# Fused attention and gated MLP on one core: the half tile of keys fed one row group at a time

## Chip, core and metric

One NeuronCore of a Trainium2 chip runs the whole program. The metric is the device time of one execution in microseconds (us). All times of the kernel before and its trace below are of this chip.

## What is computed

```python
q_n = q / (norm(q) + 1e-6);  k_n = k / (norm(k) + 1e-6)      # (8, 12, 448, 64) each
attn = softmax(q_n @ k_n.T / tau)                            # tau = 0.1
x = (attn @ v).transpose(0, 2, 1, 3).reshape(3584, 768)
h = x @ w_in                                                 # (768, 2048)
out = (h * cos(h)) @ w_out                                   # (2048, 768)
```

There are 8 batches of 12 heads, 448 queries and keys of 64 values each. Each batch gives 448 rows of `x`, which go through the two matrix products of the MLP.

## The kernel before, in words

**Work units.** A group `g` is a pair of heads of one batch; there are 48 groups, 6 to a batch. Three groups make a unit `u` (16 units, two to a batch). The 448 keys of a head stand as 7 tiles of 64. Three pairs of tiles fill 128 partitions each; the seventh tile, the half tile of keys, has only 64 keys, so its queries are split: partitions 0 to 63 hold its keys against one half of the queries, partitions 64 to 127 the same keys against the other half.

**Scores and exponentials.** For a group, `scores(g, 0)` (L728) computes the half tile's scores, 4 matmuls of 64x64 tiles with 224 columns; `scores(g, 1)` to `scores(g, 3)` (L720) the pairs, 4 matmuls with 448 columns each. ScalarE takes each result through `exp` into the buffer `PX` (L735), which is double: group `g` uses `PX[g % 2]`, with the half tile's part in the same buffer.

**Attention product and sums.** `attend(g, direct, stages)` has three stages.
- Stage 0 and stage 1 are the half tile (`rest`, L750 to L763; I call them **R0** and **R1**). Each is 4 matmuls of 64x64 tiles with 224 columns, one in every tile of the array. R0 puts the value product of partitions 0 to 63 into one PSUM bank and, with a weight of ones, the row sums of partitions 64 to 127 into the next; R1 does it the other way round. R1 waits until R0 has finished (`settled`), because the two write the same bank from different rows of the array.
- Stage 2 is the three pairs, in tiles of 128 rows by 32 columns (**the 32-column block**): 12 matmuls for the values (`av`, L768), then for groups that are not "direct" 4 with 448 columns (`sm`, L776) and 4 with 224 columns (`sm2`, L784) for the sums. `sm2` gives each of two column tiles one half of the queries.

**Sums of groups that are not direct.** After stage 2, one copy takes values and sums to `xu` in SBUF. `chain(u)` then, once per unit: gathers the sums by two DMAs on SyncE's queue (L889), adds the two parts and takes the reciprocal on VectorE (L901, L904), writes it to DRAM ("spread", L905), reads it back to all partitions ("bcast", L907), and GpSimd multiplies the values by it (L911), which gives `xT`, the input of the first MLP product.

**MLP.** `m1(b, ...)` (L919) is the first product of batch `b` in full 128x128 tiles, followed by sine and multiply into `gT`. The second product is cut into small steps that fill the time between attention blocks: `m2_quarters` (L1017), each step 4 matmuls of 64x64 tiles with 384 columns, one in every tile of the array. Within a step the order was: for each half of the output rows `x`, first row group `z` = 0, then `z` = 1. After half of an output tile, the two row groups change PSUM banks, and the next step waits for the last one to have finished (`settled` again).

**What sets the order.** TensorE's order from group 19 on is written by hand (`PLAN["script"]`): `s20.1` is a scores step of group 20, `f4` is 4 steps of the second MLP product, `a20`, `b20`, `c20` are stages 0, 1, 2 of group 20, `m2` is the first MLP product of batch 2. Earlier groups follow `pair`. The other engines are ordered at build time by a planner (`Program.play`), which simulates all engines with costs written in the code and takes at each engine the ready operation that is due first. The array changes between three tilings: 64x64 (scores, R, second product), 128x32 (stage 2), and 128x128 (first product).

Of the kernel before, what the change touches and what calls it, by code (L numbers as in the profile page):

```python
# [6 lines left out]
ACT = mybir.ActivationFunctionType  # L7
ALU = mybir.AluOpType
F32 = mybir.dt.float32
# [9 lines left out]
    "swapped": {},  # L19
    "script": {19: """  # L20
# [8 lines left out]
        s32.1 f2 a31 f2 b31 s32.2 f5 s32.3 f7 a32 s33.0 f5 s33.1 f5 s33.2 f6 b32 c32 s33.3 f10 m4 f6  # L29
        a33 s34.0 f8 s34.1 f8 b33 c33 s34.2 f5 s34.3 f5 s35.0 f6 s35.1 f5 s35.2 f4 s35.3 f4 a34 f3 b34 s36.0 c34 c35  # L30
        s36.1 a35 f3 b35 f1 s36.2 f6 s36.3 f6 a36 s37.0 f5 s37.1 f5 s37.2 f6 b36 c36
        s37.3 f4 s38.0 f4 s38.1 f4 s38.2 f4 s38.3 f4 a37 f2 b37 s39.0 c37 c38 s39.1 a38 f3 b38 f1 s39.2 f3 s39.3 f3 m5 c39
        a39 f4 s40.0 b39 f4 s40.1 f4 s40.2 f2 s40.3 f2 s41.0 s41.1 f4 s41.2 f5 s41.3 f5 a40 f2 b40 s42.0 c40 c41
        s42.1 a41 f3 b41 f1 s42.2 f4 s42.3 f4 s43.0 f4 s43.1 f4 s43.2 f5 s43.3 f5 a42 f2 b42 s44.0 c42 c43
        s44.1 f2 a43 f2 b43 s44.2 f5 s44.3 f7 a44 s45.0 f5 s45.1 f5 s45.2 f6 b44 c44 s45.3 f10 o012 m6 f6 s46.0 a45 f12 s46.1 b45 f4 c45 s46.2 f3 s46.3 f4
# [380 lines left out]
def bass_cosine_attention__then__act_gcu_kernel(  # L416
# [13 lines left out]
    UP = 3  # L430
# [13 lines left out]
    NT = 3  # L444
    TD, LT = PLAN["turned"], 9
# [27 lines left out]
    lnn = sbs("lnn", 2, [128, UH * NB], F32)  # L473
# [4 lines left out]
    PX = sbs("PX", 2, [128, NB * S], BF16)  # L478
    xu = sb("xu", [128, 5 * UP * S], F32)
    RB = sbs("RB", 2, [128, UP * S], F32)  # L480
    sums = sbs("sums", 2, [128, 2 * SPR], F32)
    rcp = sbs("rcp", 2, [128, SPR], F32)
# [3 lines left out]
    zt = sb("zt", [128, S], BF16)  # L486
    ones = sb("ones", [128, 128], BF16)
    iot = cosb[0].bitcast(I32).ap()[:, 0:128]
# [17 lines left out]
    PXv = [t.ap()[:, 0 : NT3 * 2 * S].rearrange("p (c a s) -> p c a s", c=NT3, a=2) for t in PX]  # L506
    PHv = [t.ap()[:, NT3 * 2 * S : NB * S].rearrange("p (a s) -> p a s", a=2) for t in PX]
    xuv = xu.ap().rearrange("p (r g s) -> p r g s", r=5, g=UP)
# [15 lines left out]
    HALF = 0.096  # L524

# [49 lines left out]
    pool(lambda e: e.memset(ones.ap().rearrange("p (x y) -> p x y", y=32)[:, 0:4:3], 0.0), (), ["zeros"], 0.12)  # L575
    sel = [gT.bitcast(F32).ap()[:, (f * RING + S) // 2 : (f * RING + S) // 2 + 128] for f in (NF - 2, NF - 1)]
# [65 lines left out]
    lnnv = [t.ap().rearrange("p (h s) -> p h s", h=UH) for t in lnn]  # L642
    rnv = [t.ap().rearrange("p (h s) -> p h s", h=UH) for t in rn]

    def rnorm(u, p0, p1, t=(0, 1)):
# [5 lines left out]
        if u in PLAN["roots"] or (u, p0) in PLAN["roots"]:  # L651
# [6 lines left out]
        act(lambda e: e.activation(lnnv[i][:, h, w], n2v[i][:, h, w], ACT.Ln, bias=cst.ap()[:, 1:2]),  # L658
            [("n2", i, p, z) for p, z in keys] + ["cst1"], [("lnn", i, p, z) for p, z in keys],
            n, "E", 1, "ln" + tag)  # L660
        act(lambda e: e.activation(rnv[i][:, h, w], lnnv[i][:, h, w], ACT.Exp, scale=-0.5),  # L661
            [("lnn", i, p, z) for p, z in keys], [("rn", i, p, z) for p, z in keys], n, "E", 0, "rn" + tag)
# [47 lines left out]
    def scores(g, c, bank=None):  # L710
# [5 lines left out]
        def full(e):  # L716
            for o in range(2):
                for a in range(2):
                    r = slice(64 * a, 64 * a + 64)
                    m = e.matmul(ph[BP * o : BP * o + BP, a, 0:S], t[r, c - 1 + (NT3 + 1) * o, 0:BP],  # L720
                                 t[r, :, BP : 2 * BP], start=True, stop=True)
            return m

        def half(e):
            for o in range(2):
                for a in range(2):
# [8 lines left out]
        act(lambda e: e.activation(PHv[j] if c == 0 else PXv[j][:, c - 1], ph[:, :, 0:n], ACT.Exp, scale=1.0 / TAU),  # L735
            keys, [("PX", j, c)], 2 * n, "E", label="exp%d.%d" % (g, c))

    opened, held, turned = {}, {}, set(PLAN["swapped"])

    def attend(g, direct, stages=(0, 1, 2)):  # L740
# [8 lines left out]
        folded, swapped = g in PLAN["folded"], g in turned  # L749

        def rest(e, n):
            for k in range(2):
                o = n ^ k
                r = slice(BP * o, BP * o + BP)
                for a in range(2):
                    w = vav[y][r, 2 * p + a, 0 if o else VS - 1, :] if k == 0 else ones.ap()[r, ws]
                    to = AVq[64 * a : 64 * a + 64, k, :, o, :]
                    if folded and k:
                        w = ones.ap()[r, 64 - 64 * o : 128 - 64 * o]
                        to = av_[64 * a : 64 * a + 64, 1, 0 : S // 2]  # L760
                    m = e.matmul(to, w, PHv[j][r, a, :],  # L761
                                 start=(n == 0 and g not in PLAN["quarters"] and not swapped), stop=(n == 1 and swapped))
            return m  # L763
# [8 lines left out]
        def sm(e):  # L772
            for n in range(2):
                for a in range(2):
                    o = 64 * a + 32 * n
                    t = e.matmul(av_[o : o + 32, 1, 0:S], ones.ap()[:, 32:64], PXv[j][:, n, a, :],  # L776
                                 start=swapped, stop=False)
            return t

        def sm2(e):  # L780
            for n in range(2):
                for a in range(2):
                    o, w = 64 * a + 32 * n, slice(S // 2 * n, S // 2 * n + S // 2)
                    t = e.matmul(av_[o : o + 32, 1, w], ones.ap()[:, 32:64], PXv[j][:, 2, a, w],  # L784
                                 start=False, stop=not swapped)
            return t
# [32 lines left out]
        for n in stages:  # L819
            if n < 2:  # L820
                o = P.op("PE", lambda e, n=n: rest(e, n), [("va", y), ("PX", j, 0), "ones", "zeros"], both_keys,
# [17 lines left out]
        if not direct:  # L839
            if 2 in stages:  # L840
                P.op("PE", sm, ["ones", ("PX", j, 1), ("PX", j, 2)], [ks], cost=MM, mode="C32", label="S%d" % g)
                P.op("PE", sm2, ["ones", ("PX", j, 3)], [ks], cost=HALF, mode="C32", label="S%d" % g)
# [3 lines left out]
            both = bass.AP(xu, (u % 3 * UP + p) * S, [[5 * UP * S, 128], [(3 + i - u % 3) * UP * S, 2], [1, S]])  # L846
# [9 lines left out]
        if folded:  # L856
            s, r = xuv[:, 3 + i, p, 0 : S // 2], RBv[i][:, p, 0 : S // 2]
# [14 lines left out]
        act(lambda e: e.activation(xuv[:, 3 + i, p, :], av_[:, 1, 0:S], ACT.Ln), [ks], [("xs", i, p)], S, "E",  # L872
            label="lnS%d" % g, bias=PLAN["bs"] if g < PB else 0.0)
        act(lambda e: e.activation(r, xuv[:, 3 + i, p, :], ACT.Exp, scale=-1.0), [("xs", i, p)], [("RB", i, p)], S, "E",  # L874
# [10 lines left out]
    def chain(u):  # L885
        i, b = u % 2, u // 2
        n = sum(UP * u + p not in PLAN["direct"] for p in range(UP))
        w = SPR // UP * n
        dma("SP", [lambda e, r=r: e.dma_start(  # L889
            sums[i].ap()[:, w * r : w * r + w],  # L890
# [462 lines left out]
```

## Time and profile before

| | us |
|---|---|
| three timed executions | 420.59, 421.1, 423.0 |
| their median | 421.1 |
| the profiled execution | 420.54 |
| span of its trace | 418.8 |

The span is from the first to the last instruction of the trace; the profiled execution takes 1.7 us more than its span. A row of the timeline has start, duration, engine, line, operation, output and inputs with shapes, and the number of merged instructions. The duration of a matmul in the trace runs from its start to its modelled end, and consecutive matmuls overlap; what a block costs TensorE is the time from its start to the start of the next block.

### The profile page before, as it was taken

Reading aid. Unit: us, or ns where it says so; the run is one execution under the profiler, and the core shown is the slowest. Engines: PE = TensorE matmul, PEld = TensorE weight load, DVE = VectorE, ACT = ScalarE, POOL = GpSimd, SP = SyncE. Lnnn points to the kernel's source line nnn. Section 1 sums busy time; section 2 is a strip of 40 time slices with the busy share of each in tenths; the row PEclk is TensorE's granted clock in tenths of the full one; section 3 lists DMA queues with packets and bytes.
Section 4 is the critical chain, followed back from the end, with each engine's and each line's share of the span. In section 5 each row is a group of like instructions: output and inputs, shape, how many; then the busy total and the mean of one; then the engine's idle time right before and its main releaser. Section 6 shows DMA issues by size and latency. Waiting matters only on the chain.

```text
span 418.8 us, 13571 instructions
## 1 busy us (share of the span) xinstructions
PE 409.6 (98%) x6074; PEld 236.5 (56%) x6074; DVE 189.5 (45%) x250; ACT 271.3 (65%) x363; POOL 242.7 (58%) x193
## 2 busy tenths in 40 slices
PE   7899999999999999999999999999999999999997
PEld 3354556655556555665466555665566655565565
DVE  3564744456663277124753087213862244223421
ACT  5887578983987746877498556776498745703500
POOL 4999977989761666938864782907867320020000
PEclk9999999999999999999999999999999999999999
DMA  8999999879849997579766993949966720141023
GB/s 191 251 253 226 209 223 172 213 174 198 144 104 151 207 222 185 109 168 217 168 114 127 210 242 83 147 109 212 212 123 128 161 68 3 41 121 38 2 67 85
DMA packets 80254, 63.61 MB, mean 152 GB/s; under 512 B 44996, under 2 KB 75204, under 8 KB 80196
## 3 DMA queue, kind: packets, MB, share of 16 engines
q1 hardware_dynamic: 61988, 50.06, 55.4%
q0 software_dynamic: 18048, 12.59, 20.2%
q8 instruction: 48, 0.79, 0.8%
q10 hardware_dynamic: 160, 0.10, 0.1%
q14 instruction: 10, 0.08, 0.1%
HBM read 54.98 MB, written 11.13 MB: 158 GB/s over the span
## 4 chain that ended last, share of the span: by engine, by line
PE 92%; ACT 4%; POOL 1%; DVE 1%; DMA 1%; issue 1%; SPq 0%; ACTq 0%; POOLq 0%
PE MP L1017 27%; PE SC L919 21%; PE AV L919 11%; PE SC L720 6%; PE AV L768 4%; PE MP L1046 4%; PE SC L1046 3%; PE SC L768 2%; PE AV L761 2%; PE AV L794 2%; PE MP L919 2%; ACT PX L735 2%; PE SC L728 1%; ACT cosb L948 1%; PE MP L809 1%; PE AV L1046 1%
## 5 line engine op out<-in xcount | busy, mean ns | idle before, releaser
L735 ACT ACTIVATE PX<-SC 128x896 bf16<-128x896 f32 (+1 forms) x166 | 132.8, 828 | 26.1 <-PE SC L720 18.2
L1017 PE MATMUL MP<-W,gT 64*64 64x384 bf16 x2816 | 142.3, 324 | 0.9 <-DVE qkT L707 0.6
L1017 PEld LDWEIGHTS MP<-W,gT 64*64 64x64 bf16 x2816 | 79.2, 107 | 35.7 <-PE MP L1017 3.8
L919 PE MATMUL SC<-xT,W 128*128 128x448 bf16 x468 | 94.9, 353 | 0.0
L669 POOL TENSOR_TENSOR qks<-raw,rn 128x896 bf16<-128x896 f32 (+1 forms) x48 | 79.8, 1679 | 24.6 <-ACT rn L661 24.0
L630 POOL TENSOR_TENSOR sq<-raw 128x896 bf16<-128x896 f32 x44 | 73.6, 1692 | 9.0 <-DMA raw<-in_q_dram 7.0
L948 ACT ACTIVATE cosb<-SC,cst 128x896 f32<-128x896 f32 x39 | 39.1, 1006 | 57.0 <-PE SC L919 52.6
L911 POOL TENSOR_TENSOR xT<-xu,RB 128x448 bf16<-128x448 f32 x34 | 37.8, 1136 | 60.7 <-DMA RB<-scr 60.7
L919 PEld LDWEIGHTS SC<-xT,W 128*128 128x128 bf16 x468 | 45.5, 98 | 42.8 <-ACT xu L848 0.6
L950 DVE TENSOR_TENSOR gT<-SC,cosb 128x896 bf16<-128x896 f32 x39 | 42.4, 1089 | 40.6 <-ACT cosb L948 38.3
L919 PE MATMUL AV<-xT,W 128*128 128x448 bf16 x264 | 56.7, 353 | 0.0
L984 DVE COPY osb<-MP 128x384 f32<-128x384 f32 x50 | 25.8, 553 | 66.8 <-PE MP L1017 56.1
L637 DVE TENSOR_REDUCE n<-sq 128x14 f32<-128x896 bf16 (+2 forms) x49 | 51.2, 1058 | 6.1 <-ACT sq L628 5.3
L720 PE MATMUL SC<-qkT 64*64 64x448 bf16 x504 | 45.6, 356 | 0.6 <-ACT PX L735 0.6
L919 PEld LDWEIGHTS AV<-xT,W 128*128 128x128 bf16 x264 | 25.6, 98 | 24.2 <-ACT xu L848 0.3
L948 ACT ACTIVATE cosb<-AV,cst 128x896 f32<-128x896 f32 x22 | 22.1, 1006 | 23.6 <-PE AV L919 20.7
L950 DVE TENSOR_TENSOR gT<-AV,cosb 128x896 bf16<-128x896 f32 x22 | 23.9, 1088 | 14.3 <-ACT cosb L948 14.2
L604 POOL DMA_DIRECT2D va<-in_v_dram x32 | 21.9, 692 | 7.0 <-DMA raw<-in_q_dram 4.2
L878 POOL TENSOR_TENSOR xT<-xu,RB 128x448 bf16<-128x448 f32 x8 | 9.1, 1134 | 28.5 <-ACT RB L874 28.5
L851 DVE COPY xu<-AV 128x896 f32<-128x896 f32 x13 | 14.2, 1091 | 21.5 <-PE AV L784 14.6
L552 ACT ACT_TABLE_LOAD x17 | 21.8, 1283 | 1.0 <-PEq L1335 0.7
L720 PEld LDWEIGHTS SC<-qkT 64*64 64x64 bf16 x504 | 14.4, 106 | 14.2 <-ACT PX L735 6.1
(95 smaller groups left out, 428.0 us busy)
## 6 DMA issues: line engine op xcount, KB each, us to landing
raw<-in_k_dram SPq DMA_DIRECT2D x48, 224.0 KB, 6.5
raw<-in_q_dram SPq DMA_DIRECT2D x48, 224.0 KB, 6.7
out_dram<-osb SPq DMA_DIRECT2D x54, 192.0 KB, 3.5
va<-in_v_dram POOLq DMA_DIRECT2D x32, 192.0 KB, 7.1
RB<-scr SPq DMA_DIRECT2D x18, 336.0 KB, 4.7
W<-in_moe_w_in_dram POOLq DMA_DIRECT2D x4, 768.0 KB, 15.9
W<-in_moe_w_out_dram POOLq DMA_DIRECT2D x4, 768.0 KB, 18.6
RB<-scr SPq DMA_DIRECT2D x6, 224.0 KB, 4.0
```

The source lines that it names most:

```text
L630: pool(lambda e, x=x, y=y: e.tensor_tensor(y, x, x, ALU.mult), src_, dst, 0.1 + n * 1.78e-3, label="sq%d.%d" % (u, p)).pad = LATE if u > 1 ...
L637: dve(lambda e, w=w: e.tensor_reduce(out=n2v[i][:, 2 * p : 2 * p + 2, w], in_=sqv[p][:, :, w, :], axis=mybir.AxisListType.X, op=ALU.add), ...
L669: f = lambda e, s0=s0, s1=s1: e.tensor_tensor(qksv[i][:, p, s0:s1].rearrange("p s h d -> p h s d"), rawv[i][:, h, s0:s1, :], bass.AP(rn[i] ...
L720: m = e.matmul(ph[BP * o : BP * o + BP, a, 0:S], t[r, c - 1 + (NT3 + 1) * o, 0:BP], t[r, :, BP : 2 * BP], start=True, stop=True)
L735: act(lambda e: e.activation(PHv[j] if c == 0 else PXv[j][:, c - 1], ph[:, :, 0:n], ACT.Exp, scale=1.0 / TAU), keys, [("PX", j, c)], 2 * n ...
L911: pool(lambda e, p=p: e.tensor_tensor(xTv[b % 2][:, UP * i + p, :], xuv[:, u % 3, p, :], RBv[i][:, p, :], ALU.mult), [("RB", i, p), ("xa", ...
L919: t = e.matmul(ph[:, a, 0:S], W1v[:, order[c], 128 * n : 128 * n + 128], xTv[b % 2][:, order[c], :], start=(c == 0), stop=(c == NKC - 1))
L948: act(lambda e, ph=ph, cz=cz: e.activation(cosv[cz], ph[:, :, 0:S], ACT.Sin, bias=cst.ap()[:, 0:1], scale=1.0), names(gi) + ["cst0"], [("c ...
L950: dve(lambda e, ph=ph, cz=cz, gi=gi: e.tensor_tensor(gTv[:, 2 * gi : 2 * gi + 2, S * (b % 2) : S * (b % 2) + S], ph[:, :, 0:S], cosv[cz], ...
L984: dve(lambda e: e.tensor_copy(dst, po[:, 0:n]), name, [("osb", o, hf)], n, label="osb%d" % t)
L1017: r = e.matmul(POH[b][x : x + 64, 0:HW], gTv[k, y, col + x : col + x + 64], W2v[k, y, HW * b : HW * b + HW], start=(y == 0 and h == 0), st ...
L1046: r = e.matmul(po[:, 0 : w[1] - w[0]], gTv[:, y, col : col + 128], W2v[:, y, w[0] : w[1]], start=(y == 0), stop=(y == NF - 1))
```

## The change

From unit 7 on (`"alone": range(7, 16)`), for the 25 groups that are not direct (21, 22, and 24 to 46), the two half-tile stages do only the value product: R0 is now 2 matmuls on partitions 0 to 63, R1 is 2 matmuls on partitions 64 to 127. The half tile's sums move to the 32-column block: a new weight `tail` (128x32: 16 columns of ones for each row group) gives the sums of both row groups in one matmul of 224 columns per head, in the column tile that used to take one half of the third pair. The third pair is redistributed, 336 columns to one column tile and 112 to the other.

```diff
+        def row(e, o):
+            r = slice(BP * o, BP * o + BP)
+            for a in range(2):
+                m = e.matmul(AVq[64 * a : 64 * a + 64, 0, :, o, :], vav[y][r, 2 * p + a, 0 if o else VS - 1, :], PHv[g % 3][r, a, :],
+                             start=(o == 0 and not swapped), stop=(o == 1 and swapped))
+            return m
         def sm(e):
+            w = ones.ap()[:, 80:112] if alone else ones.ap()[:, 32:64]
-                    t = e.matmul(av_[o : o + 32, 1, 0:S], ones.ap()[:, 32:64], PXv[j][:, n, a, :],
-                                 start=swapped, stop=False)
+                    t = e.matmul(av_[o : o + 32, 1, 0:S], w, PXv[j][:, n, a, :], start=alone or swapped, stop=False)
+        def sm2(e):
+            for a in range(2):
+                e.matmul(AVq[64 * a + 32 : 64 * a + 64, 1, :, 0, :], tail.ap(), PHv[g % 3][:, a, :], start=False, stop=False)
+            for a in range(2):
+                e.matmul(av_[64 * a : 64 * a + 32, 1, 0:SH], ones.ap()[:, 80:112], PXv[j][:, 2, a, 0:SH], start=False, stop=True)
+            for a in range(2):
+                t = e.matmul(av_[64 * a + 32 : 64 * a + 64, 1, SH:S], ones.ap()[:, 80:112], PXv[j][:, 2, a, SH:S],
+                             start=False, stop=True)
+            return t
+            if n < 2 and alone:
+                o = P.op("PE", lambda e, n=n: row(e, n), [("va", y), ("PH", g % 3)], [ka], cost=HALF - 0.006 if n else 0.008,
+                         mode="Q", label="R%d" % g)
+                if n:
+                    P.settled(opened[g], o)
```

Here `SH` is 336. The old `sm2` stays as `sm1` for the other groups. The sums of the second row group now lie in partitions 48 to 63 of each 64, in the places of the first half of the queries. A third gather DMA reads them, shifted by 32 columns (two zeroed gaps in `xu` make the shift safe), and the addition runs over three parts:

```diff
-            bass.AP(xu, (32 * r * 5 + 3 + i) * UP * S, [[64 * 5 * UP * S, 2], [w, 64], [1, w]]))
-            for r in range(2)], [("xs", i, p) for p in range(n)], [("sums", i)], "sums%d" % i, 0.7,
+            sums[i].ap()[:, w * r : w * r + w], bass.AP(xu, x, [[64 * XW, 2], [w, 64], [1, w]]))
+            for r, x in enumerate((XS[i], 32 * XW + XS[i], 48 * XW + XS[i] - HQ)[:m])], ["gap"] + [("xs", i, p) for p in range(n)], [("sums", i)], "sums%d" % i, 0.7,
```

For all groups, the order inside a step of 64x64 tiles becomes row group 1 (partitions 64 to 127) first, then row group 0:

```diff
-            for o in range(2):
-                for a in range(2):
+            for a in (1, 0):
+                for o in range(2):
...
-                for x in range(0, 128, 64):
-                    for z in range(2):
+                for z in (1, 0):
+                    for x in range(0, 128, 64):
```

The half tile's exponentials get a buffer of their own with three copies (`PH[g % 3]`). To make room, the buffer `lnn` goes (the logarithm is written to `rn`), `rcp` becomes single, and the zeros for the warm-up matmuls lie in an output buffer. Five small memsets are added at the start on VectorE. In the hand-written order four places change:

```diff
-        s32.1 f2 a31 f2 b31 s32.2 f5 s32.3 f7 a32 s33.0 f5 s33.1 f5 s33.2 f6 b32 c32 s33.3 f10 m4 f6
-        a33 s34.0 f8 s34.1 f8 b33 c33
+        s32.1 f2 a31 f2 b31 s32.2 f5 s32.3 f2 a32 f5 b32 s33.0 f5 s33.1 f5 s33.2 f6 c32 s33.3 f10 m4 a33 f6
+        b33 s34.0 f8 s34.1 f8 c33
...
-        a39 f4 s40.0 b39 f4 s40.1 f4 s40.2 f2 s40.3 f2 s41.0 s41.1 f4 s41.2 f5 s41.3 f5
+        a39 f4 s40.0 b39 f4 s40.1 f4 s40.2 f4 s40.3 f2 s41.0 f2 s41.1 f3 s41.2 f3 s41.3 f4
...
-        s44.1 f2 a43 f2 b43 s44.2 f5 s44.3 f7 a44 s45.0 f5 s45.1 f5 s45.2 f6 b44 c44 s45.3 f10 o012 m6 f6 s46.0 a45 f12 s46.1 b45 f4 c45
+        s44.1 f2 a43 f2 b43 s44.2 f5 s44.3 f4 a44 f3 b44 s45.0 f5 s45.1 f5 s45.2 f6 c44 s45.3 f10 o012 m6 a45 f6 b45 s46.0 f12 s46.1 f4 c45
```

More of the change, by code (lines that the diff above doesn't have):

```diff
@@ L19 @@
     "swapped": {},
+    "alone": range(7, 16),
     "script": {19: """
@@ L444, in bass_cosine_attention__then__act_gcu_kernel @@
     NT = 3
+    XS = [UP * S * (3 + i) + HQ * (i + 1) for i in range(2)]
+    XW = XS[1] + UP * S
     TD, LT = PLAN["turned"], 9
@@ L724, in half @@
         def half(e):
[L725 to L726 removed]
+            for a in (1, 0):
+                for o in range(2):
                     r = slice(64 * a, 64 * a + 64)
@@ L747, in attend @@
         ws = slice(32, 96) if direct else slice(64, 128)
-        folded, swapped = g in PLAN["folded"], g in turned
+        folded, swapped, alone = g in PLAN["folded"], g in turned, not direct and u in PLAN["alone"]
         def rest(e, n):
@@ L841, in attend @@
                 P.op("PE", sm, ["ones", ("PX", j, 1), ("PX", j, 2)], [ks], cost=MM, mode="C32", label="S%d" % g)
-                P.op("PE", sm2, ["ones", ("PX", j, 3)], [ks], cost=HALF, mode="C32", label="S%d" % g)
+                if alone:
+                    P.op("PE", sm2, ["ones", "tail", ("PH", g % 3), ("PX", j, 3)], [ks], cost=0.15, mode="C32", label="S%d" % g)
+                else:
+                    P.op("PE", sm1, ["ones", ("PX", j, 3)], [ks], cost=HALF, mode="C32", label="S%d" % g)
             if swapped and 1 not in stages:
```

85 lines of the change are left out of this document (46 added, 39 removed).

## The prediction

> **What bounds the kernel now.** I read the page first: the share of the engines, the granted clock, and the chain that ended last.
>
> ```profile
> span 418.8 us, 13571 instructions
> ...
> PE 409.6 (98%) x6074; PEld 236.5 (56%) x6074; DVE 189.5 (45%) x250; ACT 271.3 (65%) x363; POOL 242.7 (58%) x193
> ...
> PEclk9999999999999999999999999999999999999999
> ...
> PE 92%; ACT 4%; POOL 1%; DVE 1%; DMA 1%; issue 1%; SPq 0%; ACTq 0%; POOLq 0%
> ```
>
> TensorE works in 98% of the span at full clock, and it is 92% of the last chain. In the part that the change touches, a stage table has no hole at all:
>
> ```profile
> 164.00:189.00 25.00, 24.96 (x596) 15.83 (x592) 7.66 (x12) 20.95 (x31) 15.62 (x12) 1.00 0.69 150
> 189.00:236.00 47.00, 47.00 (x792) 27.75 (x788) 22.51 (x29) 34.24 (x45) 32.24 (x24) 1.00 0.84 163
> ```
>
> The first two numbers after the stage are its length and TensorE's busy time. So from unit 7 on the time is a plain sum of what each block costs TensorE, and the change is worth what it takes from this sum, unless it makes a wait. Costs of blocks come from the timeline, as the distance between starts. The first row ends group 25's 32-column block; then come group 26's block and its half tile:
>
> ```profile
> 186.79 0.27 PE L784 MATMUL SC<-PX,ones 128*32 128x224 bf16 x4
> 186.88 0.74 PE L768 MATMUL AV<-PX,va 128*32 128x448 bf16 x12
> 187.45 0.36 PE L776 MATMUL AV<-PX,ones 128*32 128x448 bf16 x4
> 187.64 0.27 PE L784 MATMUL AV<-PX,ones 128*32 128x224 bf16 x4
> 187.84 0.38 PE L720 MATMUL SC<-qkT 64*64 64x448 bf16 x4
> 188.05 0.33 PE L1017 MATMUL MP<-W,gT 64*64 64x384 bf16 x4
> 188.22 0.26 PE L761 MATMUL AV<-PX,va 64*64 64x224 bf16 x1
> ...
> 188.31 0.49 PE L1017 MATMUL MP<-W,gT 64*64 64x384 bf16 x8
> 188.64 0.26 PE L761 MATMUL AV<-PX,ones 64*64 64x224 bf16 x1
> ...
> 188.73 0.36 PE L720 MATMUL SC<-qkT 64*64 64x448 bf16 x4
> ```
>
> Read the starts. 187.45 to 187.64: 448 columns cost 0.19, so a column costs 0.42 ns. 188.31 to 188.64: two steps of 384 columns cost 0.33. R0 (188.22) and R1 (188.64) cost 0.09 each, which is 224 columns: 0.095. The 224 columns of `sm2` cost 0.09 before another block of the same tiling (186.79) and 0.20 before a change of tiling (187.64), so a change costs 0.11.
>
> **The change part by part.**
>
> *The half tile.* R0 and R1 used all four tiles for 0.095 each. Now each uses one row group. R0 occupies row group 0 for 0.095, while the next step can enter row group 1 at once; from there row group 0 runs 0.095 behind, until R1 occupies row group 1 for 0.095 and they are level. If the row groups can part, the pair costs 0.095 and not 0.19. The trace of before has no lag of this size; the nearest rows are these:
>
> ```profile
> 110.75 0.39 PE L720 MATMUL SC<-qkT 64*64 64x448 bf16 x4
> 110.94 0.26 PE L761 MATMUL AV<-PX,ones 64*64 64x224 bf16 x1
> 110.97 0.26 PE L761 MATMUL AV<-PX,va 64*64 64x224 bf16 x1
> ```
>
> One tile starts its part of a block 0.03 before the others start theirs, so tiles are not tied together. I take the full saving: 25 groups x 0.095 = 2.38 less. The two added starts stand in the queue ahead of the next step; starts in a block lie some 0.0035 apart (four of them within 0.01 at 188.22), so 25 x 0.007 = 0.18 back. From above the bound is no saving at all (rival 2).
>
> *The sums.* The column tile that gets `tail` runs 224 + 112 = 336 columns, the other 336 at once, where both ran 224. That is 112 columns, 0.047, and two more starts, 0.007: 25 x 0.054 = 1.35 more. The weights of the 112 columns could be late; a weight load takes 0.11, which would be 25 x 0.11 = 2.7 at most. The nearest row is against it: at 186.79 to 186.88 new weights followed 224 columns in the same 32-column tiles without a gap. I take 0. From below, it can't be less than the columns. The number of changes of tiling is the same in both orders of TensorE's instructions (106), so those cancel.
>
> *R1's wait.* R1 waits for R0's end. The weight loads show when it is released:
>
> ```profile
> PEld AV L761 <- PE AV L761: 2.2, 10, 0.2
> 188.22 0.21 PEld L1017 LDWEIGHTS MP<-W,gT 64*64 64x64 bf16 x8
> 188.55 0.11 PEld L761 LDWEIGHTS AV<-PX,va 64*64 64x64 bf16 x2
> ```
>
> In this window of two steps, R1's weights came 0.33 after R0's start, 0.09 before TensorE reached R1 at 188.64, which hid the load. Now the leading row group reaches R1 0.33 after R0, just when the load begins. Queued behind R1 are its own matmuls and the next scores step, whose exponential ScalarE waits for. The cost lies between 0 and a load of 0.11; a load that begins late costs 0.02 at 187.84 to 188.05 (0.21 where 448 columns take 0.19). I take 0.035. Of the 25 windows between R0 and R1, 9 have two steps: 9 x 0.035 = 0.3 (bounds 0 and 1.0). With three steps or more the load is in time.
>
> *Windows that lose the lag.* Any wait of the whole array between R0 and R1 lets the lagging row group catch up, and then R1 costs its full 0.095. One window (group 36) has a change of banks of the second product inside, which waits for the lagging row group: 0.1. Four more have scores inside; no wait of before stands there long enough to count.
>
> *Order inside a step.* Row group 1 first, for scores and the second product. R0 and R1 already went row group by row group and cost exactly their columns, so 0.
>
> *The gather.* A third DMA on SyncE's queue, in 9 units. The case with least room is unit 7, for batch 3's first product:
>
> ```profile
> 174.51 1.18 SPq L889 DMA_DIRECT2D sums<-xu  x2
> 177.49 1.23 SPq L686 DMA_TRANSPOSE qkT<-qks  x1
> 178.77 0.58 SPq L905 DMA_DIRECT2D scr<-rcp  x1
> 180.75 1.18 SPq L988 DMA_DIRECT2D out_dram<-osb  x2
> 181.98 1.23 SPq L907 DMA_DIRECT2D RB<-scr  x2
> 177.33 0.24 DVE L904 RECIPROCAL rcp<-rcp 128x14 f32<-128x14 f32 x1
> 189.93 2.22 POOL L911 TENSOR_TENSOR xT<-xu,RB 128x448 bf16<-128x448 f32 x2 [8.11 <-DMA RB<-scr]
> 193.09 0.54 PE L919 MATMUL AV<-xT,W 128*128 128x448 bf16 x2
> ```
>
> One more gather is 1.18 / 2 = 0.59. The reciprocal would end at 177.57 + 0.6 = 178.2, and its spread stands behind the transpose until 178.72 anyway. The read-back stands behind an output whose place the change does not move. So 0 here, and were all 0.6 passed on, the second `xT` would end at 192.15 + 0.6, before its matmul at 193.09. In other units the delay passes through, but they have more room. Past the gather, the transposes and loads behind it move by 0.6. The addition over three parts is a few hundredths. The price if this cover goes is rival 3.
>
> *The start.* Five memsets come before the first reduction; they are off the path:
>
> ```profile
> 0.89 0.06 DVE L572 MEMSET cst<- 128x1 f32 x1
> 1.59 0.24 DVE L1075 MEMSET zt<- 128x224 uint32 x1
> 5.94 0.70 DVE n L637
> ```
>
> Five times 0.06 moves the zeros from 1.83 to 2.1; the first link of VectorE in the last chain is at 5.94, behind the first load. Cost 0. Sharing `rcp` and `rn` adds order between operations that already lie in order; a third half-tile buffer can only take waits away. 0 for both.
>
> **Sum.** -2.38 + 0.18 + 1.35 + 0.3 + 0.1 = -0.45, against the profiled execution's 420.54 (span 418.8 and 1.7 around it): 420.1. The median of the runs shown, 421.1, is 0.56 above the profiled one; on its footing the forecast is 421.1 - 0.5 = **420.6**. Twice as many columns leave the half tile as come to the sums (224 against 112), but small terms eat half of it.
>
> **Rivals.**
>
> 1. *The forecast*, 420.6; its own range, with the terms' nearer bounds (-0.85 with nothing lost, +0.3 with late weights in all nine) and the scatter of the runs, is 419.6 to 421.6. Chance 0.64.
>
> 2. *The change does not do what it says: row groups do not part.* A step would wait for R0 in all tiles. The pair costs 0.19 as before, the sums and starts still cost 1.35 + 0.18: 421.1 + 1.5 = 422.6. For it: no lag over 0.03 is in the trace. Against it: 0.03 is there. Chance 0.10.
>
> 3. *The sums come late to the first product (slower).* Place: SyncE and GpSimd between gather and `xT`, units 7 and 11. It decides once the second `xT` of unit 7 is over 193.09 - 192.15 = 0.94 later. The gather alone does not do that; a further GpSimd instruction pushed ahead does:
>
> ```profile
> L669 POOL TENSOR_TENSOR qks<-raw,rn 128x896 bf16<-128x896 f32 (+1 forms) x48 | 79.8, 1679 | 24.6 <-ACT rn L661 24.0
> 285.05 3.32 POOL L911 TENSOR_TENSOR xT<-xu,RB 128x448 bf16<-128x448 f32 x3 [13.14 <-DMA RB<-scr]
> 289.90 0.35 PE L919 MATMUL SC<-xT,W 128*128 128x448 bf16 x1
> ```
>
> With 1.68 + 0.6, batch 3 waits 1.3, and batch 5, whose room is 289.90 - 288.37 = 1.5, waits 0.8: 420.6 + 2.1 = 422.7; a second such push would make it 425. For it: GpSimd's order of these two kinds does change, in later units. Against it: there the first product is further off. Chance 0.13.
>
> 4. *Weights of the lagging row group can't load during R0.* In the rows above, second-product weights began to load at 188.22, as R0 entered the same tiles, and the step started at 188.31, so they do. If they did not, each window would pay a load of 0.107 (the second product's mean) in the row group that sets the end: 25 x 0.107 = 2.7, hence 420.6 + 2.7 = 423.3. Chance 0.03. The Trainium skill, TensorE: Matmul & The Clock Gate, Part 3 (What overlaps and what doesn't), says that weight loads overlap matmuls in flight only where the row group differs; by that rule this rival would hold, and the trace disagrees.
>
> 5. *More than the sum.* Nothing lost (-0.85), and the third half-tile buffer removes some of TensorE's waits for exponentials:
>
> ```profile
> PEld SC L720 <- ACT PX L735: 6.1, 20, 0.5
> ```
>
> This is idle time of weight loads, most of it hidden; a tenth of it would be 0.6: 421.1 - 1.5 = 419.6. Chance 0.10.
>
> **How the numbers follow.** The likeliest is 420.6. The range takes rival 5 with some scatter below, rivals 2 and 3 above: 419.0 to 422.9; rival 4 and a doubled rival 3 stay out. About 0.5%, 2.1 us, is what a measurement of this kernel can tell from no change. Faster by more needs rival 5 and then some: 0.08. Slower by more needs rival 4, or the upper part of 2 and 3: 0.13. Within: 0.79.
>
> **What would show it.** Right: after R0 (two matmuls) the next step's rows come split, two and two, 0.09 apart, until R1; `sm2`'s block costs 0.25 to the next start where it cost 0.20; in windows of two steps R1's weights start as its matmuls do. Wrong: a step starting whole 0.09 after R0 (rival 2); holes on TensorE ahead of the first product at batches 3 or 5 (rival 3); 112-column matmuls starting over 0.11 after the `tail` ones.

## The result, and the profile after

| | before | after |
|---|---|---|
| median of 21 runs each, us | 421.1 (420.56 to 423.0) | 420.51 (420.09 to 421.71) |
| ratio, with its 95% interval | | 0.9982 [0.9974, 0.999] |
| the profiled execution, us | 420.54 | 421.53 |
| its span, us | 418.8 | 419.7 |

The change made the kernel 0.6 us faster by the medians; the interval of the ratio makes it 0.4 to 1.1. The forecast was 420.6. The two profiled executions say the opposite (419.7 against 418.8), and that has to be settled first. The page of after:

```profile
span 419.7 us, 13486 instructions
...
PE 410.3 (98%) x6024; PEld 240.4 (57%) x6024; DVE 190.1 (45%) x255; ACT 271.6 (65%) x363; POOL 242.8 (58%) x193
...
PE 92%; DMA 4%; ACT 2%; DVE 1%; issue 0%; POOL 0%; SPq 0%; ACTq 0%
```

TensorE still works in 98% of the span. But DMA is 4% of the last chain, where it was 1%. The longest piece of that chain says why (start, duration, what):

```profile
6.35 11.97 DMA va<-in_v_dram
```

One load of values took 12 us, at the very start, before any group that the change alters. So I cut each trace at the first matmul of batch 2's first product. Up to there, from the start of the span, four profiled executions of the two kernels took 143.91 and 143.56 (before), 145.22 and 143.77 (after): the start varies by 1.5 us for one and the same kernel. From there on almost nothing varies. I call the time from that matmul to the start of the last one **the stage**. It took 271.58 and 271.57 in before, 271.25 and 271.25 in after. The stage is a far sharper meter than the times, and it says that the change brings **0.33 us** there.

Where in the stage? The stage table of before, by batches (columns: stretch, its length, TensorE's busy time and matmuls, then the other engines), one line a batch, the last from batch 6's first product to the end of the span:

```profile
143.91:190.06 46.15, 46.11 (x753) 26.68 (x749) 20.93 (x27) 32.39 (x43) 29.86 (x26) 1.00 0.87 178
190.06:237.00 46.94, 46.94 (x789) 27.84 (x785) 22.51 (x29) 34.16 (x44) 33.11 (x25) 1.00 0.84 163
237.00:286.11 49.11, 49.11 (x837) 29.18 (x833) 21.42 (x27) 31.41 (x40) 26.53 (x20) 1.00 0.80 153
286.11:333.35 47.24, 47.05 (x788) 27.80 (x784) 22.75 (x29) 34.01 (x44) 34.24 (x27) 1.00 0.83 164
333.35:418.80 85.45, 82.39 (x740) 47.29 (x736) 28.26 (x38) 29.47 (x32) 6.66 (x6) 1.00 0.22 55
```

The same of the second trace of after:

```profile
143.77:189.94 46.17, 46.12 (x742) 27.35 (x738) 20.93 (x27) 32.40 (x43) 30.71 (x26) 1.00 0.90 180
189.94:236.92 46.98, 46.98 (x776) 28.57 (x773) 22.52 (x29) 34.24 (x44) 31.44 (x23) 1.00 0.81 157
236.92:285.98 49.06, 49.06 (x825) 29.96 (x821) 21.61 (x27) 31.29 (x40) 28.28 (x23) 1.00 0.81 159
285.98:332.96 46.98, 46.98 (x777) 28.59 (x773) 22.71 (x29) 34.04 (x44) 33.45 (x26) 1.00 0.83 166
332.96:418.30 85.34, 82.31 (x736) 47.78 (x732) 28.41 (x38) 29.42 (x32) 7.27 (x7) 1.00 0.22 55
```

If 25 half tiles each saved the same, the gain would lie evenly. It doesn't: +0.02, +0.04 and -0.05 in the first three batches, then -0.26 in one, and -0.07 from there to the last matmul (the last lines run on to the end of the span). And in the batch with -0.26 before had a hole (47.24 long, 47.05 busy) that after has not. The hole is here, in before:

```profile
308.82 0.27 PE L728 MATMUL AV<-qkT 64*64 64x224 bf16 x4
309.27 0.38 PE L720 MATMUL SC<-qkT 64*64 64x448 bf16 x4 [0.19 <-ACT PX L735]
```

A scores step starts 0.45 behind a half tile's scores that cost 0.1: it waits for ScalarE's exponential. In after, two steps of the second product stand between them (`s41.0 f2 s41.1`, where before had `s41.0 s41.1`). That is the redistributed line of the hand-written order, and not the half tile at all.

The half tile itself did on the array what the prediction said. Group 26 in after, TensorE's timeline (the group whose rows of before the prediction shows):

```profile
188.92 0.31 PE L809 MATMUL AV<-PX,ones 128*32 128x336 bf16 x1
188.93 0.26 PE L807 MATMUL AV<-PH,tail 128*32 128x224 bf16 x1
188.93 0.31 PE L809 MATMUL AV<-PX,ones 128*32 128x336 bf16 x1
188.93 0.26 PE L807 MATMUL AV<-PH,tail 128*32 128x224 bf16 x1
189.02 0.22 PE L811 MATMUL AV<-PX,ones 128*32 128x112 bf16 x2
189.17 0.38 PE L730 MATMUL SC<-qkT 64*64 64x448 bf16 x4
189.38 0.49 PE L1052 MATMUL MP<-W,gT 64*64 64x384 bf16 x6
189.56 0.26 PE L778 MATMUL AV<-PH,va 64*64 64x224 bf16 x2
189.65 0.49 PE L1052 MATMUL MP<-W,gT 64*64 64x384 bf16 x6
189.88 0.28 PE L778 MATMUL AV<-PH,va 64*64 64x224 bf16 x2
189.97 0.37 PE L730 MATMUL SC<-qkT 64*64 64x448 bf16 x4
```

From 188.92 to 189.17 the sums cost 0.25 where before had 0.20. R0 (189.56, now two matmuls) lies inside a run of three steps, one ahead of it and the two of the window: six matmuls of the second product from 189.38, R0, six more. The step in which R0 falls is split two and two, its second half 0.10 behind its first (189.55 and 189.65; the view merges the first half into the row at 189.38). From 189.38 to the next scores step at 189.97 it is 0.59; in before, 188.05 to 188.73, it was 0.68.

I added up all stretches of the stage, each from the first matmul of one tiling to the first of the next. The 32-column blocks grew by 1.23 us (25 x 0.049). The 64x64 stretches shrank by 1.56. The stretch of the hole shrank by 0.345, and its like two batches earlier, where the order did not change, by 0.045; I put the difference, 0.30, down to the line of the order. Full tiles: 0. So the half tile saved 1.26, the sums cost 1.23, and the line of the order brought 0.30.

### The profile page after: what moved, and what is told of

It is laid out like the page before. It is cut to its first block, busy times and chain, and to the rows that moved or that the text cites. A ratio compares the mean times of both kernels' runs of the same rounds, so it can differ in the third digit from the quotient of the medians.

```text
span 419.7 us, 13486 instructions
## 1 busy us (share of the span) xinstructions
PE 410.3 (98%) x6024; PEld 240.4 (57%) x6024; DVE 190.1 (45%) x255; ACT 271.6 (65%) x363; POOL 242.8 (58%) x193
## 4 chain that ended last, share of the span: by engine, by line
PE 92%; DMA 4%; ACT 2%; DVE 1%; issue 0%; POOL 0%; SPq 0%; ACTq 0%
PE MP L1052 28%; PE SC L954 21%; PE AV L954 11%; PE SC L730 6%; PE AV L785 4%; PE MP L1081 4%; DMA va<-in_v_dram 3%; PE SC L1081 3%; PE SC L785 2%; PE AV L821 2%; PE MP L954 2%; PE AV L771 1%; PE SC L738 1%; PE AV L730 1%; PE MP L836 1%; PE AV L1081 1%
## 5 line engine op out<-in xcount | busy, mean ns | idle before, releaser
L745 ACT ACTIVATE PX<-SC 128x896 bf16<-128x896 f32 x125 | 112.3, 918 | 19.7 <-PE SC L730 17.2
L1052 PEld LDWEIGHTS MP<-W,gT 64*64 64x64 bf16 x2816 | 83.1, 107 | 34.2 <-PE MP L1052 4.8
L745 ACT ACTIVATE PH<-SC 128x448 bf16<-128x448 f32 x39 | 21.3, 546 | 4.8 <-PE SC L738 4.4
L887 DVE COPY xu<-AV 128x896 f32<-128x896 f32 x12 | 13.1, 1092 | 20.5 <-PE AV L801 8.8
```

The source lines that it names most:

```text
L745: act(lambda e: e.activation(PHv[g % 3] if c == 0 else PXv[j][:, c - 1], ph[:, :, 0:n], ACT.Exp, scale=1.0 / TAU), keys, [("PX", j, c) if ...
L1052: r = e.matmul(POH[b][x : x + 64, 0:HW], gTv[k, y, col + x : col + x + 64], W2v[k, y, HW * b : HW * b + HW], start=(y == 0 and h == 0), st ...
```

## The experiments

All compare with the changed kernel's stage, 271.25, and the kernel before's, 271.58. Stretches that an edit does not touch agree between runs within some 0.01 us.

| kernel | median, us | ratio to before, 95% interval | stage, us |
|---|---|---|---|
| f1, before again | 420.3 (one run) | | 271.57 |
| f2, after again | 420.09 (one run) | | 271.25 |
| g1, before with the new line | 420.44 | 0.9992 [0.9981, 1.0003] | 271.27 |
| g2, after with the old line | 420.72 | 0.9991 [0.9982, 0.9999] | 271.49 |
| e1, order inside a step as before | 420.29 | 0.9987 [0.9978, 0.9996] | 271.31 |
| e2, four tiles | 422.21 | 1.003 [1.0016, 1.0044] | 272.65 |
| e3, no `tail` | 419.95 | 0.9976 [0.9965, 0.9986] | 270.39 |
| e4, paired scores | 422.11 | 1.0033 [1.002, 1.0046] | 273.21 |
| e5, hand-over filled | 419.72 | 0.9974 [0.9965, 0.9984] | 270.70 |
| e6, three steps | 420.15 | 0.9982 [0.9973, 0.9991] | 271.11 |
| e7, e5 and e6 | 419.72 | 0.9975 [0.9962, 0.9988] | 270.49 |
| e8, two gathers | 420.5 (one run) | | 271.74 |

**e1: does the new order inside a step do the work?** All three 64x64 loops get their old order back, the rest of the change stays.

```diff
-            for a in (1, 0):
-                for o in range(2):
+            for o in range(2):
+                for a in range(2):
...
-                for z in (1, 0):
-                    for x in range(0, 128, 64):
+                for x in range(0, 128, 64):
+                    for z in range(2):
```

> The changed kernel with the order inside a step of 64x64 tiles as before (scores: output half outside, head inside; second product: x outside, z = 0 then z = 1 inside). Theory A, matmuls start strictly in the order of the program: a step behind R0 now begins with a matmul of row group 0, which must wait 0.095 for R0 and holds up those of row group 1 behind it, so no lag builds up, the pair costs 0.19 again and most of the half tile's saving goes: 1.5 to 2.4 us more than the changed kernel, 422 to 423. Theory B, each row group takes its matmuls in its own order: the order inside a step does not matter, 420.5 within 0.4, and the split of steps after R0 stays in the trace.

The stage is 271.31, 0.06 more. TensorE's timeline of e1 still shows the split around R0:

```profile
178.74 0.26 PE L738 MATMUL SC<-qkT 64*64 64x224 bf16 x2
178.75 0.26 PE L778 MATMUL AV<-PH,va 64*64 64x224 bf16 x2
178.84 0.33 PE L1052 MATMUL MP<-W,gT 64*64 64x384 bf16 x2
178.84 0.26 PE L738 MATMUL SC<-qkT 64*64 64x224 bf16 x2
```

The half scores' one row group starts with R0, the other 0.10 later, beside the next step's first half. Each row group takes its own matmuls in its own order, so the order between row groups is worth next to nothing.

**e2: is the split what saves?** Two idle matmuls are put back into R0 and R1, on the other row group, so that each uses four tiles again (some sums are counted twice, and R0 and R1 again wait for both banks of their block, as in before).

```diff
+            r = slice(BP - BP * o, 2 * BP - BP * o)
+            for a in range(2):
+                m = e.matmul(AVq[64 * a : 64 * a + 64, 1, :, 1 - o, :], ones.ap()[r, 64:128], PHv[g % 3][r, a, :],
+                             start=(o == 0 and not swapped), stop=(o == 1))
```

> The changed kernel with two idle matmuls of 224 columns put back into R0 and R1 on the other row group, so that all four tiles are occupied again, while the sums stay in the 32-column block (some sums are counted twice in the groups that do the sums first). Theory: the saving is that of the row groups parting; what the trace shows of it after the changed kernel's losses, 1.56 us, comes back: 422.0 (421.5 to 422.9). Rival, the gain came from the new order of the other engines or the third half-tile buffer: no change, 420.5.

The stage grows by 1.40, or 0.056 for each of 25 groups. The split is real, and it is worth 0.056 a group on average, not the 0.095 of the prediction. Where a window stands alone and nothing else waits (group 38) the stretch grows by 0.096; elsewhere by less. The 1.56 that was expected back still held the 0.30 of the line of the order, which stays in e2.

**e3: what do the sums cost?** The half tile's sums are left out, and the third pair is split evenly again.

```diff
-    SH = S * 3 // 4
+    SH = S // 2
...
-            for a in range(2):
-                e.matmul(AVq[64 * a + 32 : 64 * a + 64, 1, :, 0, :], tail.ap(), PHv[g % 3][:, a, :], start=False, stop=False)
```

> The changed kernel without the tail matmuls and with the third pair cut 224 to 224 as before: the half tile's sums are left out. Theory: each of 25 blocks ends 0.049 earlier, 1.2 us less: 419.3 (418.9 to 419.8). Rival, TensorE does not set the pace there and waits for exponentials instead: 420.1 to 420.5.

Every 32-column block is 0.049 shorter again, 1.23 in all, but the stage only by 0.86. The other 0.37 comes back in eight stretches right behind such blocks, 0.049 in most of them. There the end of the block did not set the time, something else did.

**e4: what sets the time where nothing is saved?** The places without a saving were those where the second product changes its PSUM banks between R0 or R1 and a half tile's scores. If a fixed latency passes there whatever stands in between, a full scores step moved into it should be free.

```diff
-  s33.0 f5 s33.1 f5 s33.2 f6 c32
+  s33.0 s33.1 f10 s33.2 f6 c32
...
-  b33 s34.0 f8 s34.1 f8 c33
+  b33 s34.0 s34.1 f16 c33
```

and likewise `s37.0 s37.1 f10`, `s45.0 s45.1 f10`, `s46.0 s46.1 f16`.

> The changed kernel with the half tile's scores and the next scores step side by side at the five places where a change of banks of the second product follows the half tile's scores (groups 33, 34, 37, 45, 46). Theory: there the next second-product step comes 0.405 to 0.477 after the one before it however little stands between, so an R block taken away in that place saves nothing; with 0.28 of scores between them the excess of 0.147 to 0.219 goes at all five: 0.9 to 1.0 us less than the changed kernel, 419.5 (419.2 to 420.0). Rival, two scores steps so close make TensorE or a later scores step wait for ScalarE's exponential: the gain is lost, 420.3 to 421.

Slower, by 1.96 us in the stage. Groups 33 and 45 gained 0.14 each as hoped, and group 37 0.03. Groups 34 and 46 lost 1.13 each, by a wait that I had not named. The timeline of e4 at group 34, with VectorE's row between TensorE's:

```profile
256.75 0.27 PE L738 MATMUL SC<-qkT 64*64 64x224 bf16 x4
...
256.87 1.09 DVE L985 TENSOR_TENSOR gT<-SC,cosb 128x896 bf16<-128x896 f32 x1
...
258.10 0.38 PE L730 MATMUL SC<-qkT 64*64 64x448 bf16 x4 [1.09 <-DVE gT L985]
```

These two groups follow a first product. The scores step now stood before VectorE had read that product out of the bank (256.87 + 1.09 = 257.96), and TensorE stood still for it.

**e5: the same idea without that bank.** All 16 steps of a bank go in one run, and in groups 34 and 46 the scores step stands behind it.

```diff
-  s33.0 f5 s33.1 f5 s33.2 f6 c32
+  s33.0 s33.1 f16 s33.2 c32
...
-  b33 s34.0 f8 s34.1 f8 c33
+  b33 s34.0 f16 s34.1 c33
```

and the same for groups 45 and 46; group 37 as in e4.

> The changed kernel with scores moved into the second product's hand-overs, none of them right behind the first product: groups 33, 37 and 45 keep the half tile's scores beside the next ones at the change of banks; the later scores of groups 33, 34, 45 and 46 move in front of the 32-column block that stands in a change of output tile. Theory: at a change of banks the next step comes 0.405 after the last, at a change of tile 1.53 (VectorE's two copies lie between), whatever stands there; filling them gives 0.14, 0.03 and 0.14 as the run before showed, and about 0.09 at each of four changes of tile: 0.6 to 0.7 us less than the changed kernel, 419.8 (419.3 to 420.3). Rival, scores that come earlier or later make TensorE wait for a PSUM bank, as they did right behind the first product: 420.3 or more.

The stage is 0.55 shorter than after's: 0.14 in each of two places, 0.03 in group 37, and 0.062 at each of the four changes of output tile, where about 0.09 was expected. TensorE's timeline of e5 at group 33 shows a whole scores step where only the wait had been:

```profile
230.62 0.28 PE L738 MATMUL SC<-qkT 64*64 64x224 bf16 x4
230.72 0.37 PE L730 MATMUL AV<-qkT 64*64 64x448 bf16 x4
230.91 2.60 PE L1052 MATMUL MP<-W,gT 64*64 64x384 bf16 x58
```

From the half scores to the next step it is now 0.29, with a scores step of 0.19 inside; in after it is 0.22 with nothing inside (rows in the next section).

**e6: what do windows of two steps lose?** In the nine windows one step is moved in from before R0, so that R1's weights have three steps.

```diff
-  s26.3 f3 a25 f2 b25
+  s26.3 f2 a25 f3 b25
```

> The changed kernel with R0 one second-product step earlier in the nine windows that had two steps, so that all have three. Theory: R1's weights no longer begin to load when TensorE is already there; each of nine windows gets back the 0.02 that it lost: 0.2 us less, 420.3, seen in the trace as R1 to the next block 0.096 to 0.10 where it was 0.112 to 0.120. Rival, the late start is that of the scores behind R1, not of R1: no change in the trace.

0.15 shorter, near the 0.2 expected, but not in the way expected: four windows (groups 25, 30, 37, 42) give back 0.037 each and the other five nothing. R1 is no longer late in any of the nine. Behind 26, 28 and 40 the next scores wait for ScalarE instead, and behind 31 and 43 comes a hand-over of banks (both in the next section).

**e7: both edits together.**

> The changed kernel with both rearrangements of the two runs before. If the two theories hold and don't meet in one place: 0.8 to 0.9 us less than the changed kernel, 419.6 (419.1 to 420.2). If TensorE then waits elsewhere for ScalarE or VectorE: 420.3 or more.

The stage is 0.76 shorter than after's, a little more than the two parts (0.55 + 0.15): with the hand-overs filled, windows 31 and 43 give back 0.02 each as well. Its ratio to before is 0.9975 [0.9962, 0.9988]; that it also beats after rests on the stage, since the intervals of the two ratios overlap.

**e8: does the third gather cost anything?** It is left out (so the second row group's half-tile sums are missing).

```diff
-            w, m = SPR // UP * n, 3 if u in PLAN["alone"] else 2
+            w, m = SPR // UP * n, 2
```

> The changed kernel without the third gather and its part of the addition, so that the sums of the half tile's second row group are left out. Theory, the third gather hides behind what stands on SyncE's queue and before the first product: the stages from unit 7 on take the same time within 0.1 us. Rival, it delays the first product of some batch: those stages are 0.3 us or more shorter.

Nothing became shorter. All stretches agree with after's within 0.01 but one, which is 0.49 longer, just before batch 3's first product:

```profile
187.64 0.38 PE L730 MATMUL SC<-qkT 64*64 64x448 bf16 x4
188.42 0.51 PE L1052 MATMUL MP<-W,gT 64*64 64x384 bf16 x6 [0.40 <-issue]
```

"issue" means that TensorE waited for nothing that the profile shows. What it was stays open. Without the gather the planner also put some operations of VectorE and GpSimd in another order (the first of them at 224 us), and no stretch shows that either. In this one execution the gather costs nothing that can be seen.

**f1, f2: is the 0.33 chance?** Both kernels once more, unchanged.

> The kernel before once more, unchanged, for its trace. Theory (the program from batch 2's first product on is fixed, and what varies between executions is the start): from the first matmul of batch 2's first product to the last matmul 271.58 us within 0.05, as in the first trace of before; the way up to there anywhere in 141.4 to 143. Rival (this part varies as much as the start does, so that the 0.33 us between the two traces is chance): off by 0.2 or more.

> The changed kernel once more, unchanged, for its trace. Theory: from the first matmul of batch 2's first product to the last matmul 271.25 us within 0.05; up to there 141.4 to 143, no longer than before's by rule. Rival (this part varies by 0.2 or more): off by that. If the start is longer than before's again by 0.5 or more (142.9 against 142.0), the five memsets at the start would have a price after all.

The stages repeat within 0.01. The expectations count the way up to there from the first matmul, which stands at 1.90 in before and 2.30 in after; so counted it is 141.67 and 141.47, both inside 141.4 to 143. The first matmul does come 0.4 later in after, with the five memsets ahead of it (the prediction had 0.3), but the start of after, now 143.77, is as long as before's (143.91 and 143.56). The long start of its first trace is not a cost of the change, and a price of the memsets doesn't show; with starts that vary by 1.5, a price of some tenths could not be seen.

**g1, g2: how much of it is the one line?** The line of groups 39 to 41 alone, put into before, and taken back from after.

```diff
-  a39 f4 s40.0 b39 f4 s40.1 f4 s40.2 f2 s40.3 f2 s41.0 s41.1 f4 s41.2 f5 s41.3 f5
+  a39 f4 s40.0 b39 f4 s40.1 f4 s40.2 f4 s40.3 f2 s41.0 f2 s41.1 f3 s41.2 f3 s41.3 f4
```

> The kernel before with one line of the hand-written order as in the changed kernel: the steps of the second product between groups 40 and 41 redistributed, so that two stand between the half tile's scores and the scores step behind them, where none stood. Nothing else of the change. Theory X (most of what the change brought is this line: in the trace of before that scores step waits 0.27 us there for ScalarE's exponential, and that stretch alone is 0.30 shorter than its like in the changed kernel): from the first matmul of batch 2's first product to the last matmul 271.58 - 0.30 = 271.28 us, which is the changed kernel's 271.25. Rival Y (the wait went with the change's own buffers for the half tile's exponentials, or the line only moves it): 271.5 or more.

> The changed kernel with that one line as it was before. Theory X: the wait comes back, 271.25 + 0.30 = 271.55 us, no shorter than the kernel before's 271.58 by more than 0.05: row groups, sums and late weights together bring nothing that a run can tell. Rival Y (the third buffer or the row groups took the wait away): 271.25 to 271.35.

(The stretch is 0.30 longer in before than in the changed kernel; the first expectation says it the other way round.) Before with this line alone has a stage of 271.27: 0.31 of the 0.33 without one half tile changed. The place in g1, where before had its hole:

```profile
309.25 0.27 PE L728 MATMUL AV<-qkT 64*64 64x224 bf16 x4
309.34 0.49 PE L1017 MATMUL MP<-W,gT 64*64 64x384 bf16 x8
309.67 0.36 PE L720 MATMUL SC<-qkT 64*64 64x448 bf16 x4
```

After without it has 271.49: 0.24 back, not 0.30. So the rest of the change takes 0.06 of that wait by itself, and all of it together, the line aside, brings 0.02 (beside the new line) to 0.09 (beside the old one).

## Why the number was right, and the steps behind it were not

The forecast of 420.6 came out (420.51), and its sum, -0.45, is near the stage's -0.33. But two of its steps are wrong and cancel: it had -1.80 for the half tile, +1.35 for the sums and nothing for the order, and measured were -1.26, +1.23 and -0.30. That the total came out is luck.

**The step that was missing: the moved steps.** The prediction puts no price on the four places where the hand-written order changes. One of them is worth 0.31 (g1), about all that the change brings in the stage. The wait that it removes was in the trace of before, as the row at 309.27 above; the stage table from which the prediction read "no hole at all" ended at 236, long before the last of the 25 groups. The other three places were not tried by themselves, so whatever they cost or bring is inside the 1.26 of the half tile. Its rival 5 had the right releaser, ScalarE's exponential for a scores step, but gave the credit to the third half-tile buffer; g2 leaves at most 0.06 for that.

**The step that was mis-sized: "Windows that lose the lag".** The prediction counts one such window, 0.1, and says of four more that "no wait of before stands there long enough to count". The half tile saved 1.26, where its terms came to -2.38 + 0.18 + 0.3 + 0.1 = -1.80. Of the 25 x 0.095 = 2.38, then, 1.12 was lost:

- The nine windows of two steps lose 0.2, where the prediction took 0.3: 0.15 comes back with a third step (e6), and 0.04 more once the hand-overs are filled (e7). The rows show it as it was forecast: R1's weights start to load as its matmuls should (189.88 here and in group 26's row of R1 above), and the scores behind follow late. Weight loads of after:

```profile
189.39 0.11 PEld L778 LDWEIGHTS AV<-PH,va 64*64 64x64 bf16 x2
189.55 0.21 PEld L1052 LDWEIGHTS MP<-W,gT 64*64 64x64 bf16 x6
189.88 0.10 PEld L778 LDWEIGHTS AV<-PH,va 64*64 64x64 bf16 x2
```

- The hand-over is the largest part, at a change of banks above all. Group 33's half scores with what stands ahead of them, in before (group 32's R0), then in after (its R1, moved there by the new order):

```profile
230.64 0.26 PE L761 MATMUL SC<-PX,ones 64*64 64x224 bf16 x1
230.73 0.27 PE L728 MATMUL SC<-qkT 64*64 64x224 bf16 x4
230.88 0.36 PE L1017 MATMUL MP<-W,gT 64*64 64x384 bf16 x4
```

```profile
231.62 0.56 PE L1052 MATMUL MP<-W,gT 64*64 64x384 bf16 x8
231.94 0.26 PE L778 MATMUL SC<-PH,va 64*64 64x224 bf16 x2
232.02 0.28 PE L738 MATMUL SC<-qkT 64*64 64x224 bf16 x4
232.24 1.01 PE L1052 MATMUL MP<-W,gT 64*64 64x384 bf16 x20
```

  Half scores cost 0.095, but the step behind them came 0.15 later in before, and 0.22 later in after: it waits for the last step of the other bank. From the start of that step to the next one before had 0.405 at twelve of the stage's fifteen changes of banks, whether a scores step stood between or R0 with the half scores; at the other three longer work or the wait at 309.27 stood there. So R0's columns cost nothing there, and fewer of them save nothing. In after it is 0.46 here (231.62 + 0.16 to 232.24), because the lagging row group ends later. Five groups stand so (33, 34, 37, 45, 46): four have 0.46 to 0.48 in after, one still 0.405. In before only 0.05 of it stood open behind the work that hid the rest, and that is why the prediction passed over it. e5 fills these places, and the changes of output tile, and gets 0.55 back. The stretches in which these hand-overs lie hold ten windows (31 to 36, 43 to 46); of their 0.95, 0.46 was saved and 0.04 is that of windows 31 and 43, so some 0.45 was lost to hand-overs.
- ScalarE was, as it seems, the next limit in some places. At group 30 in after the half scores start 0.22 behind the R1 ahead of them (group 28's), where R1 costs 0.1, and the exponential that would free their bank ends 0.15 before they start, at 216.52 + 0.95 = 217.47:

```profile
216.52 0.95 ACT L745 ACTIVATE PX<-AV 128x896 bf16<-128x896 f32 x1
...
217.40 0.28 PE L778 MATMUL SC<-PH,va 64*64 64x224 bf16 x2
217.62 0.29 PE L738 MATMUL AV<-qkT 64*64 64x224 bf16 x4
```

  Groups 30 and 42 lose 0.12 so, and group 27 0.075. This is read from the trace, where the profile names no releaser for so short a wait, and was not tried by itself.
- One window was lost to a wait that the trace of before shows. Group 23's half scores stand between R0 and R1 of group 22, and in before they start 0.30 behind an R0 that costs 0.09:

```profile
168.49 0.26 PE L761 MATMUL AV<-PX,ones 64*64 64x224 bf16 x1
...
168.76 0.14 PEld L728 LDWEIGHTS SC<-qkT 64*64 64x64 bf16 x4 [0.32 <-issue]
168.79 0.29 PE L728 MATMUL SC<-qkT 64*64 64x224 bf16 x4
```

  In after it is 0.30 again (169.76 to 170.06): the whole array waits, no lag is left for R1 to make good, and the window saves nothing. The prediction's "no wait of before stands there long enough to count" was a misreading here. What the wait is for, the profile does not say.

Together these come to some 1.06 of the 1.12.

**The terms that held.** The sums: +1.35 forecast, +1.23 measured; the extra starts cost nothing to be seen (0.049 a block, where 112 columns are 0.047). The added starts at R0 and R1 (+0.18) are not in the trace either: windows in which nothing waits save 0.09 to 0.097. The order inside a step: 0, measured 0.06 (e1). The gather: 0 as far as one execution shows (e8). The memsets: nothing to be seen in the start (f2).

**The rivals.** Rival 2 (row groups do not part) is out by e1's rows and by e2. Rival 3 (sums late to the first product) is out: batch 3 and batch 5 start 46.17 and 49.06 after the product before, against 46.15 and 49.11. Rival 4 (weights can't load while R0 runs in the same row group) is out: second-product weights load from 189.55 on, R0 starts at 189.56, and their step starts at 189.65. Rival 5 was right on the wait and wrong on what removes it.

The sums and the split do not add up as the prediction took them. Sums with four tiles (e2) have a stage of 272.65, the split without sums (e3) 270.39, both (after) 271.25, neither, with the new line (g1), 271.27. So the split is worth 0.88 where the sums are missing and 1.40 where they are there: what the blocks of the sums add in front of a hand-over is partly time that would be waited for anyway. (e2 and e3 also carry the change's small parts, so these are good to some 0.1.)

**What stays open.** The medians differ by 0.6, the interval begins at 0.4, and the stage holds 0.33. The rest lies ahead of batch 2's first product, in a part that varies by 1.5 us, or is scatter of the runs. For scatter speaks g1: up to group 39 its program is that of before, its stage holds 0.31, and its median too is 0.6 below that of before beside it (420.44 against 421.05). The 0.49 of e8, the three other moved places and the wait of group 23's half scores are open as well.

## What to carry to other kernels

A busy time of 98% does not make every column cost its time: where work stands inside a fixed latency (a change of banks, an exponential that frees a bank), it is hidden, and removing it brings nothing; measure from the last step of the old bank to the first of the new one, in every place, before multiplying a saving by a count. Price every moved step of a change too, and look for the wait that stood where it lands: here one line of reordering brought what the redesigned tile did not. And where the start of a program varies by more than the effect, cut the traces at a fixed instruction: behind it two executions here agreed within 0.01 us in 271.

## What the runs showed of the hardware

Row groups of the array keep their own order, and so matmuls start out of program order. In the rows of e1 above, R0 (L778) stands ahead of all four of the half scores' matmuls (L738) in the program, and two of these start 0.01 us before it. And the first of the half scores in the program is one of row group 0: it starts at 178.84, 0.10 behind the two of row group 1 at 178.74. (The view does not name the row group of a matmul; that the late two are row group 0's is read from R0, which stands in row group 0 at 178.75.)

The Trainium skill, TensorE: Matmul & The Clock Gate, Part 3 (What overlaps and what doesn't), says that matmuls start and end strictly in program order. The trace disagrees, by the 0.01 and the 0.10 above. The lag of one row group behind the other, 0.09 to 0.10 in the rows above, holds over several steps, until R1 or a wait of the whole array.
